# Windowed attention scores from 256-query strips and shared half tiles, in a two-layer transformer kernel on one Trainium2 core

## The chip, the cores and the metric

The kernel runs on one core of one Trainium2 chip. The metric is the device time of one execution in microseconds (us). A core has engines that run side by side and wait for one another by semaphores: TensorE (PE) multiplies matrices, ScalarE (ACT) does exponentials and GELU, VectorE (DVE) copies, adds and normalises, GpSimd (POOL) does masks and small work, SyncE (SP) issues the DMAs. PE's results go to PSUM, eight banks of 128 partitions x 512 float32.

## The reference

Two layers on x, 2048 tokens by 576, in bfloat16. Each layer adds an attention block and an MLP block, both behind a layer norm (each branch normalises twice on the MLP side):

```python
H = 32; Dh = D // H; W = 256            # 32 heads of 18
scores = jnp.einsum("bhqd,bhkd->bhqk", q, k) * (Dh ** -0.5)
mask = (idx[:, None] - idx[None, :] >= 0) & (idx[:, None] - idx[None, :] < W)
p = _softmax(jnp.where(mask[None, None], scores, -1e9), axis=-1)
o = jnp.einsum("bhqk,bhkd->bhqd", p, v)          # then @ wo
h = _gelu(jnp.einsum("bsd,df->bsf", y, w1) + b1) # F = 4608
return jnp.einsum("bsf,fd->bsd", h, w2) + b2
```

A query sees its own position and the 255 before it. Seen from a tile of 128 keys, the queries that matter run from the tile's first token to 255 tokens past its last: 384 queries, of which the first 128 and the last 128 are triangles.

## The kernel before, in words

The 2048 tokens are cut into chunks of 512 (four tiles of 128 queries). Two layers give eight chunks, k = 0 to 7. Per chunk there are: `qkv` (projections, L835 in the 64x128 array shape), `E` (attention, in three parts of 3, 3 and 2 head groups), `tail` (output projection, L1070), `G_part` (first MLP layer with GELU, three parts, L1115 and ACT L1125) and `mm2` (second MLP layer, three parts). The stages of chunk k's attention are interleaved with those of chunk k-1's MLP.

**Attention.** The 32 heads are eight groups g of four. A head has 18 channels in a 32-row strip, so four heads fill the array's rows: a score matmul (L923) has 32 rows and 128 columns of weights (a key tile), and the four of a group run side by side, each into its own PSUM bank. For a group, `units_of` lists three units of 512 score columns (six segments of 128, 256 or 384 queries, 12 blocks of 128 x 128 in all). A unit goes through `scores`: 8 matmuls, two exponentials (L933, two heads each, 1,024 elements a partition) into a slot of `pT` (six slots), and masks by affine_select on POOL (L954) over each diagonal or far-edge block. Chunks 0 and 4 start a layer, so they have no earlier tiles: nine blocks a group, and in chunk 4 the ninth blocks of four groups share one unit (`scores9`). `pv` (L975) multiplies the 12 blocks with V: 24 matmuls of 128 rows x 20 columns, four heads side by side, one PSUM bank for a group. V carries a column of ones, so the sum of a row comes with it, and DVE divides (L986 to L992). The first chunk has its own routine `E0`, which issues the first unit of three groups ahead.

**Array shapes.** PE's work comes in four shapes: full (128x128), 64-row halves (`qkv`, `tail`, `G_part`), 32-row quarters (scores) and 32-column quarters (`pv`). `mm2` may be issued as full matmuls (L775) or as four column quarters (L778, `quad`); it takes quarters where it stands in one run with `pv`, so that the shape need not change there.

**Order.** Nothing runs in source order. A planner (`Plan.schedule`) gives every task a cost and a latency written in the source, and picks the next by earliest start and then by priority; a change of shape costs `SWITCH`. A table `PL.nudge` adds a number to each stage's priority, and `PL.turn` holds back tasks that would change the shape. The result is one fixed instruction list per engine. Where the planner sees PE idle for over 0.4 us in the first 140 us, `keep_warm` puts in matmuls on a zero tile (L671), whose result nobody reads.

Of the kernel before, what the change touches and what calls it, by code (L numbers as in the profile page):

```python
# [8 lines left out]
ALU = mybir.AluOpType  # L9
# [426 lines left out]
def build_kernel(nc, A_x, A_wqkv, A_wo, B_x, B_w1, B_b1, B_w2, B_b2, out):  # L436
# [19 lines left out]
    PVG = [()] * 8  # L456
    PVLAG = 1
# [20 lines left out]
    PL.turn = {"hc": 0.3, "rh": 0.05, "rc": 0.05, "ch": 0.3}  # L478
    PL.nudge = {"": -1.63, "b": -20.47, "ea0.0": 108.12, "ea0.1": -112.05, "ea0.p0": -0.32, "ea0.p1": -13.77, "ea0.p2": -108.16,
# [333 lines left out]
    def qkv(k, i, prio0):  # L813
        l, t0, nt = CH[k]
        A = l * NT + t0 + i
        for n, w in enumerate("qkv"):
# [32 lines left out]
            else:  # L849
# [16 lines left out]
                if k == 0 and (w == "k"):  # L866
# [15 lines left out]
    def units_of(k):  # L882

        l, t0, nt = CH[k]
        if nt == 4:
# [3 lines left out]
        if t0 == 0:  # L889
            us = [[(0, 0, 3, 0)], [(1, 1, 3, 128)], [(2, 2, 2, 256), (3, 3, 1, 128)]]  # L890
# [467 lines left out]
```

## Time and profile before

| what | value |
|---|---|
| time, median of 3 runs | 856.21 us (855.98 to 856.74) |
| span of the profiled execution | 857.2 us |
| mean granted TensorE clock | 0.998 |
| PE busy, matmuls | 842.7 us, 12,180 |
| ACT busy | 599.1 us, of it exponentials (L933) 344.9 in 372 |
| POOL busy | 379.1 us, of it masks (L954) 282.8 in 370 |
| score matmuls (L923) | 1,248 in one group of the page, 63.2 us busy |
| PV matmuls (L975) | 1,440, 50.4 us busy |
| MLP matmuls (L1115; L775 and L778) | 291.8; 188.5 and 96.5 us busy |

The page gives no time for the profiled execution beside its span, which is 1.0 us above the median of the runs. The span is counted from the first instruction to the last. Rows of the timeline merge neighbouring instructions of one line; a row's second number reaches to the end of the last one, which lies under the first of the next row, since matmuls are pipelined. "PEld" are the weight loads, which run beside the matmuls. Matmul counts of the page may miss a few records; the listings of the program have 1,440 score matmuls.

### The profile page before, as it was taken

The page shows a single profiled execution, that of the slowest core. Times are in us where ns is not written, and L with a number is a line of the kernel's source. Part 1 is how long each engine was busy: PE and PEld are TensorE (multiplying, and loading weights), DVE is VectorE, ACT ScalarE, POOL GpSimd, SP SyncE. Part 2 cuts the span into 40 slices and gives each one's busy share as a digit, 9 for nine tenths or more (in the row PEclk, how much of TensorE's full clock was granted, in tenths as well). Part 3 has the DMA queues.
Part 4 walks back from the last instruction along what each step waited for, and adds up shares of the span by engine and source line. Part 5 has one row for each costly group of instructions (what it writes and reads, how often), then busy time and mean ns, then how long its engine had stood idle before and what let it go on. Part 6 is the DMA issues. An engine that isn't in the chain of part 4 may idle for free.

```text
span 857.2 us, 28212 instructions
## 1 busy us (share of the span) xinstructions
PE 842.7 (98%) x12180; PEld 517.6 (60%) x12180; DVE 398.6 (46%) x949; ACT 599.1 (70%) x745; POOL 379.1 (44%) x569
## 2 busy tenths in 40 slices
PE   8999999999999999999999999999999999999998
PEld 6555556556566565666665655656556556556556
DVE  6777434655257352672445723564226534162013
ACT  4988887778757787476773877748885689853730
POOL 4776554375235662263421654426534276322100
PEclk9999999999999999999999999999999999999999
DMA  7899435461596534967258443595345963346320
GB/s 198 195 184 149 127 124 145 115 165 45 166 182 124 154 94 121 186 133 191 85 124 195 89 149 122 104 223 130 112 157 116 225 187 109 119 133 186 116 84 29
DMA packets 181996, 119.86 MB, mean 140 GB/s; under 512 B 107504, under 2 KB 181872, under 8 KB 181872
## 3 DMA queue, kind: packets, MB, share of 16 engines
q1 hardware_dynamic: 181872, 118.05, 55.1%
q8 instruction: 96, 1.57, 0.8%
q14 instruction: 28, 0.23, 0.1%
HBM read 90.10 MB, written 2.36 MB: 108 GB/s over the span
## 4 chain that ended last, share of the span: by engine, by line
PE 91%; DMA 3%; DVE 2%; ACT 2%; POOL 1%; issue 1%; SPq 0%; DVEq 0%; POOLq 0%; ACTq 0%
PE ps L1115 31%; PE ps L775 25%; PE ps L778 11%; PE ps L835 8%; PE ps L923 6%; PE ps L975 5%; PE ps L1070 4%; DMA xnTm<-xn 2%; ACT pT L933 1%; DMA wqkv<-in_A_wqkv_dram 1%; PE ps L794 1%; DVE x_res L1047 1%; POOL pT L954 1%; DMA x_res<-qn 1%; DVE st_all L684 1%
## 5 line engine op out<-in xcount | busy, mean ns | idle before, releaser
L954 POOL TENSOR_SCALAR_AFFINE_SELECT pT<-pT 128x1024 bf16<-128x1024 bf16 (+1 forms) x370 | 282.8, 786 | 219.3 <-ACT pT L933 217.1
L933 ACT ACTIVATE pT<-ps 128x1024 bf16<-128x1024 f32 (+1 forms) x372 | 344.9, 999 | 42.4 <-PE ps L923 41.7
L1115 PE MATMUL ps<-xnTm,w_sb 64*128 64x512 bf16 x2592 | 291.8, 376 | 0.6 <-DVE x_res L1050 0.3
L1125 ACT ACTIVATE hT<-ps,b1col 128x512 bf16<-128x512 f32 x276 | 168.0, 688 | 176.5 <-PE ps L1115 176.4
L1115 PEld LDWEIGHTS ps<-xnTm,w_sb 64*128 64x128 bf16 x2592 | 127.5, 94 | 140.7 <-issue 4.0
L775 PE MATMUL ps<-w_sb,hT 128*128 128x288 bf16 x1410 | 188.5, 287 | 0.9 <-DVE vA L847 0.8
L1047 DVE TENSOR_TENSOR x_res<-ps,x_res 128x288 f32<-128x288 f32 x224 | 100.5, 454 | 180.7 <-PE ps L775 122.3
L775 PEld LDWEIGHTS ps<-w_sb,hT 128*128 128x128 bf16 x1410 | 130.5, 98 | 50.5 <-issue 16.9
L778 PE MATMUL ps<-w_sb,hT 128*32 128x288 bf16 x2808 | 96.5, 286 | 0.2
L835 PE MATMUL ps<-wqkv,xnTa 64*128 64x288 bf16 x1296 | 91.3, 283 | 2.2 <-DVE vA L847 0.9
L859 DVE CAST qn<-ps 128x288 bf16<-128x288 f32 x112 | 46.4, 451 | 86.4 <-PE ps L835 78.5
L986 DVE STREAM_TRANSPOSE oq<-ps 128x512 f32<-128x512 f32 x64 | 45.8, 716 | 84.6 <-PE ps L975 83.9
L778 PEld LDWEIGHTS ps<-w_sb,hT 128*32 128x32 bf16 x2808 | 72.5, 97 | 14.9 <-issue 3.4
L835 PEld LDWEIGHTS ps<-wqkv,xnTa 64*128 64x128 bf16 x1296 | 61.4, 94 | 30.0 <-issue 3.9
L923 PE MATMUL ps<-qT,kT 32*128 32x128 bf16 (+2 forms) x1248 | 63.2, 274 | 2.5 <-ACT pT L933 2.5
L697 POOL TENSOR_SCALAR vtmp<-mv_all 128x1 f32<-128x1 f32 (+2 forms) x45 | 9.2, 204 | 120.5 <-DVE mv_all L688 119.1
L1131 POOL TENSOR_TENSOR x_res<-x_res,b2bc 128x576 f32<-128x576 f32 x32 | 40.2, 1276 | 37.6 <-ACT hT L1125 37.4
L684 DVE BATCH_NORM_STATS2 st_all<-x_res 128x6 f32<-128x288 f32 (+1 forms) x128 | 53.5, 446 | 3.0 <-DMA x_res<-in_A_x_dram 2.1
L847 DVE CAST vA<-ps 128x288 bf16<-128x288 f32 x60 | 25.3, 448 | 55.1 <-PE ps L835 49.1
L975 PE MATMUL ps<-pT,vA 128*20 128x384 bf16 (+2 forms) x1440 | 50.4, 275 | 0.3 <-DVE vA L847 0.2
L923 PEld LDWEIGHTS ps<-qT,kT 32*128 32x128 bf16 x1248 | 19.2, 92 | 41.4 <-issue 26.9
L1070 PE MATMUL ps<-wo_sb,attT 64*128 64x288 bf16 x576 | 42.5, 283 | 0.3
(58 smaller groups left out, 478.4 us busy)
## 6 DMA issues: line engine op xcount, KB each, us to landing
w_sb<-in_B_w_dram SPq DMA_DIRECT2D x46, 864.0 KB, 6.1
w_sb<-in_B_w_dram SPq DMA_DIRECT2D x48, 768.0 KB, 4.8
w_sb<-in_B_w_dram SPq DMA_DIRECT2D x96, 48.0 KB, 4.6
wqkv<-in_A_wqkv_dram SPq DMA_DIRECT2D x3, 576.0 KB, 5.6
x_res<-in_A_x_dram SPq DMA_DIRECT2D x3, 576.0 KB, 4.3
wqkv<-in_B_w_dram SPq DMA_DIRECT2D x2, 864.0 KB, 5.2
out_dram<-x_res SPq DMA_DIRECT2D x12, 144.0 KB, 1.9
xnTm<-xn SPq DMA_TRANSPOSE x36, 2.8
```

The source lines that it names most:

```text
L684: add("dve", lambda e, i=i, s=s: e.bn_stats(st_all[:, t, i, :], s[:, t, i * HB:(i + 1) * HB]), reads=res, writes=[f"st{t}_{i}"], cost=0.37 ...
L775: return e.matmul(bank(b)[:, 0:HB], lhs, rhs, start=start, stop=stop, skip_group_check=True)
L778: ins = e.matmul(bank(b)[32 * j:32 * j + 32, 0:HB], lhs[:, 32 * j:32 * j + 32], rhs, start=start, stop=stop, tile_position=(0, 32 * j), sk ...
L835: ins = e.matmul(bank(bs[o])[:, 0:HB], xnTa[r:r + 64, c, i * 128:(i + 1) * 128], wqkv[r:r + 64, c, col:col + HB], start=(c == 4), stop=(ph ...
L923: ins = e.matmul(two(bs[j // 2])[:, j % 2, col:col + nq * 128], k_of(T0 + so)[0][32 * j:32 * j + 32, gg, :], qs[32 * j:32 * j + 32, gg, qo ...
L933: add("act", lambda e, h2=h2: e.activation(pT[:, sl, 2 * h2:2 * h2 + 2, lo:hi], two(bs[h2])[:, :, lo:hi], ACT.Exp, scale=SCALE), reads=[bs ...
L954: add("pool", lambda e, ap=ap, pat=pat, sgn=sgn, kind=kind: e.affine_select(ap, ap, pattern=pat, compare_op=(ALU.is_ge if kind == "d" else ...
L975: ins = e.matmul(bank(bo)[32 * j:32 * j + VW, qo * 128:(qo + nq) * 128], vA[:, (T0 + so) % VS, 8 * j + g, :], pT[:, sl, j, col:col + nq * ...
L1047: add("dve", lambda e: e.tensor_tensor(x_res[:, t, sl], bank(b)[:, 0:HB], x_old[:, t, sl], ALU.add), reads=[b] + ([f"xin{t}"] if first els ...
L1070: ins = e.matmul(bank(bs[o])[:, 0:HB], attT[r:r + 64, c, i * 128:(i + 1) * 128], wo_sb[r:r + 64, c, col:col + HB], start=(ph == 0 and c == ...
L1115: ins = e.matmul(bank(bks[i])[:, 0:n], w1_sb[r:r + 64, sls[i], col:col + 128], xnTm[r:r + 64, k % 2, c, 0:n], start=(c == 4), stop=(ph == ...
L1125: add("act", lambda e, ff=ff, hd=hd, bk=bk: e.activation(hd[:, 0:n], bank(bk)[:, 0:n], ACT.Gelu_apprx_tanh, bias=b1col[:, ff:ff + 1]), rea ...
```

## The change

**Scores.** A key tile meets only 256 queries in the full 128-key shape, from its own middle to the middle two tiles later. What is left are two triangles of 64 x 64: the tile's first 64 keys with its first 64 queries, and its last 64 keys with the 64 queries that follow the strip. The second triangle of tile i-2 and the first of tile i are put into the same 64 PSUM columns, one in partitions 0 to 63, the other in 64 to 127, by matmuls of 32 rows x 64 columns (eight side by side). Eight such pairs of triangles fill one unit, which serves two groups (four groups in chunks 0 and 4). A group then has 2.5 units of 512 columns and not 3 (chunks 0 and 4: 2.25 units, the first of 384 columns).

**Masks.** A shared unit takes two slots: POOL writes the far triangles with their mask into the second slot (`up`) and masks the near ones in place, so that each slot has zeros in the other half of the partitions. The 256-query strips have half-width triangles at both ends.

**PV.** It still runs over 128 partitions and the same columns per group (1,536; 1,152 in chunks 0 and 4): 6 segments of the two strip units and 8 segments of 64 columns from the two slots.

**Order.** A fifth shape "s" is known to the planner, with the cost `SSTEP` for its steps; `E`, `E0` and `pv` are rewritten for the new units, and the whole table of nudges is another one.

```diff
+    SSTEP = 0.045
-    PL.turn = {"hc": 0.3, "rh": 0.05, "rc": 0.05, "ch": 0.3}
-    PL.nudge = {"": -1.63, "b": -20.47, "ea0.0": 108.12, "ea0.1": -112.05, "ea0.p0": -0.32, "ea0.p1": -13.77, "ea0.p2": -108.16,
...
+    PL.turn = {"hc": 0.3, "rh": 0.05, "rc": 0.05, "ch": 0.3, "sh": 0.05, "sc": 0.05}
+    PL.nudge = {"": -251.12, "b": 5.46, "ea0.0": 2.43, "ea0.1": 0.99, "ea0.2": 1.23, "ea0.n0": 94.47, "ea0.p0": -189.64,
...
-            us = [[(0, 0, 3, 0), (-2, 0, 1, 384)], [(1, 1, 3, 128), (3, 3, 1, 0)], [(-1, 0, 2, 0), (2, 2, 2, 256)]]
...
+    def units_of(k, g):
+
+        if CH[k][1] == 0:
+            return [("", [(g, 0, 0, 5, 0), (g, 1, 2, 1, 320)]),
+                    (f"n{g}", [(g + n // 2, 2 + n % 2, 64 * n) for n in range(8)] if g % 4 == 0 else None),
+                    ("", [(g, 1, 3, 4, 0), (g, 2, 5, 3, 256), (g, 3, 7, 1, 448)])]
+        return [(f"n{g}", [(g + n // 4, n % 4, 64 * n) for n in range(8)] if g % 2 == 0 else None),
+                ("", [(g, 0, 1, 4, 0), (g, 1, 3, 4, 256)]),
+                ("", [(g, -1, 0, 3, 0), (g, -2, 0, 1, 192), (g, 3, 7, 1, 256), (g, 2, 5, 3, 320)])]
...
+                    if halves:
+                        gg, i, col = seg
+                        for h, so in ((0, i), (1, i - 2)):
+                            ins = e.matmul(two(bs[j // 2])[64 * h:64 * h + 64, j % 2, col:col + 64], k_of(T0 + so)[0][row, gg, 64 * h:64 * h + 64],
+                                           qs[row, gg, 64 * (2 * i + h):64 * (2 * i + h) + 64], start=True, stop=True, tile_position=(32 * j, 64 * h),
+                                           skip_group_check=True)
+                    else:
+                        gg, so, q, n, col = seg
+                        ins = e.matmul(two(bs[j // 2])[:, j % 2, col:col + 64 * n], k_of(T0 + so)[0][row, gg, :], qs[row, gg, 64 * q:64 * (q + n)],
+                                       start=True, stop=True, tile_position=(32 * j, 0), skip_group_check=True)
...
+    def visit(k, g, segs, prio):
+        sl = scores(k, segs, prio)
+        hs = [f"p{sl}h0", f"p{sl}h1"]
+        if len(segs[0]) == 3:
+            up = slots.popleft()
+            gs = sorted({x[0] for x in segs})
+            for n, gg in enumerate(gs):
+                cols = [x[2] // 64 for x in segs if x[0] == gg]
+                mask(sl, up, cols, -64, -1, hs, f"p{up}m{n}", prio)
+                mask(sl, sl, cols, 0, 1, hs + [f"p{up}m{n}x"], f"p{sl}m{n}", prio)
...
+            for n, (so, q, nq, sl, col) in enumerate(todo):
                 for j in range(4):
+                    ins = e.matmul(bank(bo)[32 * j:32 * j + VW, 64 * q:64 * (q + nq)], vA[:, (T0 + so) % VS, 8 * j + g, :],
+                                   pT[:, sl, j, col:col + 64 * nq], start=(n == 0), stop=(n == len(todo) - 1),
```

**Where the order moves.** PE's list at the start of chunk 6's attention: L923 are scores, L775 and L778 the second MLP layer of chunk 4 or 5, L835 projections for the next chunk. Before:

```order
L835 MATMUL ps<-wqkv,xnTa 128x288 x36
L923 MATMUL ps<-qT,kT 128x384 x4
L923 MATMUL ps<-qT,kT 128x128 x4
L775 MATMUL ps<-w_sb,hT 128x288 x24
L923 MATMUL ps<-qT,kT 128x384 x4
L923 MATMUL ps<-qT,kT 128x128 x4
L835 MATMUL ps<-wqkv,xnTa 128x288 x36
L923 MATMUL ps<-qT,kT 128x256 x8
L775 MATMUL ps<-w_sb,hT 128x288 x12
```

With the change, at the same place (L923 is now the 32x64 shape, L928 the strips, L786 the full second layer, L846 the projections):

```order
L846 MATMUL ps<-wqkv,xnTa 128x288 x36
L923 MATMUL ps<-qT,kT 64x64 x64
L786 MATMUL ps<-w_sb,hT 128x288 x12
L928 MATMUL ps<-qT,kT 128x256 x8
L786 MATMUL ps<-w_sb,hT 128x288 x12
L928 MATMUL ps<-qT,kT 128x192 x4
L928 MATMUL ps<-qT,kT 128x64 x8
L928 MATMUL ps<-qT,kT 128x192 x4
L786 MATMUL ps<-w_sb,hT 128x288 x12
```

The chunk now opens with the shared unit of groups 0 and 1, 64 short matmuls; a group then has two score runs between the MLP's pieces where it had three.

The first PV groups of the same chunk, before (L975 is PV):

```order
L975 MATMUL ps<-pT,vA 20x384 x4
L975 MATMUL ps<-pT,vA 20x128 x4
L975 MATMUL ps<-pT,vA 20x384 x4
L975 MATMUL ps<-pT,vA 20x128 x4
L975 MATMUL ps<-pT,vA 20x256 x8
L778 MATMUL ps<-w_sb,hT 32x288 x24
```

And with the change (L1025 is PV, L789 the quartered second layer):

```order
L789 MATMUL ps<-w_sb,hT 32x288 x24
L1025 MATMUL ps<-pT,vA 20x256 x8
L1025 MATMUL ps<-pT,vA 20x192 x4
L1025 MATMUL ps<-pT,vA 20x64 x8
L1025 MATMUL ps<-pT,vA 20x192 x4
L1025 MATMUL ps<-pT,vA 20x64 x32
L789 MATMUL ps<-w_sb,hT 32x288 x24
L923 MATMUL ps<-qT,kT 64x64 x64
```

A PV group has 56 matmuls where it had 24, 40 of them 64 columns wide, and a shared unit of 64 short matmuls stands one small piece of the MLP behind it.

Over the whole program PE's list has 16,366 matmuls where it had 12,180: 3,264 score and 3,264 PV matmuls for 1,440 and 1,440, 1,513 full and 3,644 quartered ones of the second layer (with chunk 1's projections) for 1,687 and 2,948, and 36 filler matmuls for the 20 of L671. The shape changes 344 times, before 393 times.

More of the change, by code (lines that the diff above doesn't have):

```diff
@@ L916, in scores @@
         bs = [Bank(SC, True), Bank(SC, True)]
+        halves = len(segs[0]) == 3
         def fn(e):
             ins = None
[L920 to L921 removed]
+            for seg in segs:
                 for j in range(4):
[L923 to L925 removed]
@@ L926, in fn @@
-            return ins
-        rd = [f"{qname}{qo + i}" for (so, qo, nq, col) in parts for i in range(nq)] + [k_of(T0 + p[0])[1] for p in parts]
-        ncol = sum(p[2] for p in parts) * 128
-        add("pe", fn, reads=rd, writes=bs, cost=0.01 + ncol * 0.00042, prio=prio, lat=0.15, alloc=bs, fifo="pa", mode="r", after=[f"p{sl}h{h}" for h in range(2)] + [f"p{sl}m{m}" for m in range(3)])
-        lo = min(p[3] for p in parts)
-        hi = max(p[3] + p[2] * 128 for p in parts)
+                    row = slice(32 * j, 32 * j + 32)
@@ L932, in scores @@
+        add("pe", fn, reads=list(dict.fromkeys(rd)), writes=bs, cost=cost, prio=prio, lat=0.15, alloc=bs, fifo="pa", mode="s" if halves else "r",
+            after=[f"p{sl}h{h}" for h in range(2)] + [f"p{sl}{m}" for m in MS])
         for h2 in range(2):
@@ L957, in scores, with runs_of @@
-        return sl
-    def pv(k, g, units, bo, first, last, prio):
-        slots.extend(sl for _, sl in units)
-        if k in SHARE and last:
-            units = units + [ninth[k, g]]
-            if g % 4 == 3:
-                slots.append(ninth[k, g][1])
+        return sl
+    def runs_of(cols):
+        out = []
+        for c in cols:
+            if out and (len(out[-1]) == 1 or c - out[-1][-1] == out[-1][1] - out[-1][0]) and not (len(out[-1]) == 1 and c - out[-1][0] > 1 and c + 1 in cols):
+                out[-1].append(c)
+            else:
+                out.append([c])
+        return out
@@ new lines, in collect @@
+    def collect(k, g, prio):
+        parts, free = [], []
+        for name, segs in units_of(k, g):
+            if name:
+                if segs is not None:
+                    kept, PL.part = PL.part, f".{name}"
+                    visit(k, g, segs, prio)
+                    PL.part = kept
+                    yield None
+                continue
+            p, f = visit(k, g, segs, prio)
+            parts += p
+            free += f
+            yield None
+        sp, ssl, n, end = side[k, g]
+        yield parts + sp, free, ssl, n, end
@@ L966, in pv @@
+    def pv(k, g, what, bo, prio):
+        todo, free, ssl, sn, end = what
+        slots.extend(free + (ssl if end else []))
         l, t0, nt = CH[k]
```

141 lines of the change are left out of this document (57 added, 84 removed), and 134 rows, old and new, of the table add.

## The prediction

> **What bounds the kernel now.** I read the page's header and slices first, then the chain of waits, then the windows by stage, then the timeline of TensorE inside one attention stage.
>
> ```profile
> span 857.2 us, 28212 instructions
> PE 842.7 (98%) x12180; PEld 517.6 (60%) x12180; DVE 398.6 (46%) x949; ACT 599.1 (70%) x745; POOL 379.1 (44%) x569
> PE 91%; DMA 3%; DVE 2%; ACT 2%; POOL 1%; issue 1%; SPq 0%; DVEq 0%; POOLq 0%; ACTq 0%
> ```
>
> TensorE (PE) sets the end: 98% busy, and 91% of the chain that ended last. A busy PE still hides gaps, so the windows come next (columns: span, then PE, weight loads, DVE, ACT, POOL busy, granted clock).
>
> ```profile
> 20.00:56.40 36.40, 32.90 (x479) 19.15 (x479) 26.74 (x67) 35.10 (x50) 28.34 (x44) 1.00 0.93 185
> 56.40:60.00 3.60, 3.60 (x49) 1.89 (x49) 2.09 (x5) 1.42 (x3) 1.91 (x4) 0.53 1.01 270
> 60.00:86.00 26.00, 24.18 (x390) 14.87 (x390) 19.02 (x47) 21.48 (x33) 17.14 (x33) 1.00 0.89 148
> 86.00:200.00 114.00, 113.66 (x1654) 66.53 (x1650) 52.19 (x126) 90.21 (x111) 58.65 (x83) 1.00 0.48 134
> 200.00:400.00 200.00, 199.92 (x3066) 123.20 (x3060) 99.73 (x235) 141.38 (x169) 93.57 (x137) 1.00 0.59 138
> 400.00:600.00 200.00, 198.25 (x3170) 123.88 (x3166) 98.40 (x232) 139.70 (x166) 86.47 (x132) 1.00 0.57 138
> 600.00:740.00 140.00, 139.18 (x2054) 83.38 (x2052) 52.39 (x117) 108.06 (x133) 65.83 (x86) 1.00 0.54 151
> ```
>
> From 86 to 740 us PE stands idle for 0.34 + 0.08 + 1.75 + 0.82 = 3.0 us in all. There only less PE work, or fewer changes of array shape, can gain. From 20 to 56.4 us ACT is busy 35.10 of 36.40 us and PE idles 3.5 us: the first chunk's attention is bound by the exponentials. At 56.4 us the clock falls to 0.53 for 3.6 us.
>
> The timeline of PE in chunk 6, whose chain of waits also gives one long run:
>
> ```profile
> 576.93 3.10 PE L775 MATMUL ps<-w_sb,hT 128*128 128x288 bf16 x24 [0.80 <-DVE vA L847]
> 579.97 0.40 PE L923 MATMUL ps<-qT,kT 32*128 32x384 bf16 x8
> 584.51 0.40 PE L923 MATMUL ps<-qT,kT 32*128 32x384 bf16 x8
> 584.84 1.64 PE L775 MATMUL ps<-w_sb,hT 128*128 128x288 bf16 x12
> 586.42 0.40 PE L923 MATMUL ps<-qT,kT 32*128 32x384 bf16 x8
> 586.74 0.83 PE L975 MATMUL ps<-pT,vA 128*20 128x384 bf16 x24
> 587.40 0.91 PE L778 MATMUL ps<-w_sb,hT 128*32 128x288 bf16 x24
> ```
> ```profile
> 240.72 4.52 PE ps L778 x144
> 771.75 11.87 PE ps L775 x96
> 783.62 23.42 PE ps L1115 x216
> 818.90 11.76 PE ps L1115 x108
> 830.66 23.64 PE ps L775 x192
> ```
>
> I price PE from start to next start. 24 full matmuls of 288 columns take 579.97 - 576.93 = 3.04 us, 96 of them 11.87; so one takes (11.87 - 3.04)/72 = 122.6 ns, and **one change of array shape** 3.04 - 24 x 0.1226 = 0.10 us. 54 pairs of 512 columns take 11.76 us, less one change 11.66, or 215.9 ns a pair. Two sizes give a **column** (215.9 - 122.6)/224 = 0.4165 ns and a **step** (matmuls that run side by side in the array) 2.7 ns more. Checks: a score unit, 512 columns, takes 0.33 us (0.213 + 0.10 + 0.013 at its second step); a PV group, 1,536 columns in 6 steps, 0.66 (0.640 + 0.016).
>
> **The change, part by part.** The counts are from the listings of the two programs.
>
> *Fewer score columns.* 360 steps with 92,160 columns become 368 steps in the 32x128 shape (63,488 columns) and 224 in the 32x64 shape (14,336, eight matmuls side by side): 77,824. 14,336 x 0.4165 ns = **-6.0 us**.
>
> *Fewer changes of shape.* The new order changes the shape 344 times, not 393, though each of the 28 shared tiles needs a shape of its own. 49 x 0.10 = **-4.9**. 174 second-layer steps go from one full matmul to four quarters: 36 quarter steps took 4.52 us with one change, 122.8 ns each against 122.6, so nothing.
>
> *More steps.* PV streams the same 92,160 columns, but in 816 steps for 360; scores have 232 more. 688 x 2.7 ns = **+1.8**.
>
> *Short steps.* 128 score steps and 576 PV steps have 64 columns, and 224 are half tiles. No row shows a step under 128 columns with several tiles. From below: 64 x 0.4165 + 2.7 = 29.4 ns. From above: the 128-column step, 56.0 ns, +26.6 each. For the instructions' pace I take the weight loads at the head of one score unit:
>
> ```profile
> 575.73 0.12 PEld L923 LDWEIGHTS ps<-qT,kT 32*128 32x128 bf16 x8 [0.24 <-issue]
> L923 PEld LDWEIGHTS ps<-qT,kT x1248: 90/91/113, 19.8 to 750.6; 32*128 32x128 bf16 x179
> ```
>
> Eight loads span 0.12 us and one lasts 0.09, so they start within some 30 ns, with four matmuls among them: 12 instructions, 2.5 ns each. A PV or score step has 8 instructions, 20 ns, below 29.4. A half-tile step has 16, 40 ns: 224 x (40 - 29.4) = **+2.4**. I add **+0.8** for the other 704 (1.2 ns each, near the lower end because the pace leaves room). Bounds for all 928: 0 to +24.7.
>
> [...]
>
> *Instruction fetch.* PE issues 2 x 16,366 instructions for 2 x 12,180.
>
> ```profile
> q8 instruction: 96, 1.57, 0.8%
> 586.00:596.00 10.00, 10.00 (x178) 6.26 (x178) 5.16 (x11) 9.31 (x11) 7.46 (x10) 1.00 0.32 50
> ```
>
> 96 packets carry 24,360 PE instructions, about 254 each; a packet's time is 0.008 x 16 x 857.2/96 = 1.14 us. Where 178 matmuls and their loads fill 10 us, a packet lasts 7 us. In the new order 64 half-tile matmuls next to a PV group of 56 are 240 instructions in some 1.1 us. If the fetch falls behind there, the loss is at most 0.25 us at each of 28 shared tiles, 7 us. I take **+1.5**. [...]
>
> *ACT.* 372 exponentials become 312.
>
> ```profile
> L933 ACT ACTIVATE pT<-ps 128x1024 bf16<-128x1024 f32 x324 | 309.7, 1023 | 38.9 <-PE ps L923 38.7
> L933 ACT ACTIVATE pT<-ps 128x768 bf16<-128x768 f32 x48 | 35.3, 837 | 3.5 <-PE ps L923 3.0
> 31.87 15.97 ACT L933 ACTIVATE pT<-ps 128x768 bf16<-128x768 f32 x22 [0.81 <-PE ps L923]
> PE ps L923 <- ACT pT L933: 2.9, 10, 0.4
> PEld ps L923 <- ACT pT L933: 13.8, 45, 0.7
> ```
>
> 44 x 1.023 + 16 x 0.837 = 58 us of ACT go, but PE waited for exponentials only 2.9 us (13.8 more are weight loads beside running matmuls), so after 86 us this is worth about nothing. In chunk 0 the pace is 15.97/22 = 0.73 us; 48 x 0.73 = 35 become 16 x 0.73 + 20 x 0.91 (1.023 less the same overlap of 0.11) = 30: 5 us off the bound engine. PE idles 3.5 us there, so no more can return, and the order puts 16 more filler matmuls (those of L671) into the first chunks, which stand where the planner saw PE without work. I take **-1.7**; bounds -7 (all idle and the low clock gone: 3.5 + 1.8 + 3.6 x 0.47) and +3 (new idle as long as before's 3.0 us from 86 us on).
>
> *POOL.* The masks cover the same 245,760 elements a partition in 416 selects for 370.
>
> ```profile
> L954 POOL TENSOR_SCALAR_AFFINE_SELECT pT<-pT 128x512 bf16<-128x512 bf16 x264 | 167.1, 648 | 189.1 <-ACT pT L933 188.1
> L954 POOL TENSOR_SCALAR_AFFINE_SELECT pT<-pT 128x1024 bf16<-128x1024 bf16 x104 | 115.8, 1113 | 28.7 <-ACT pT L933 27.6 <-PE ps L923 0.4
> PEld ps L975 <- POOL pT L954: 1.3, 6, 0.2
> ```
>
> 512 elements cost 648 ns, 512 more 465, so 183 ns are fixed and 46 selects add 8 us to an engine at 44%. PV waited for masks 1.3 us in all: cover is there, and if it went, 64 PV groups would wait.
>
> **Sum.** -6.0 - 4.9 + 1.8 + 2.4 + 0.8 + 1.5 - 1.7 = -6.1. The profiled execution's span is 857.2 us, so 851.1 there; it lies 1.0 above the median of the runs, 856.2. Forecast: **850 us**.
>
> **The rivals.**
> *Slower: short steps are bound by loads or issue, not by columns* (place: PV's 576 and the scores' 128 steps). Without its 0.8 the sum is -6.9; 6.9/704 = 9.8 ns more each, 39 ns a step, wipe it out. At 56 ns the 704 cost 18.7, the half tiles 3.6 more than taken: -6.9 + 18.7 + 3.6 = +15.4, 872 us. For it: no row has such a step. Against: PV's 128-column steps pay 2.7 ns, not more. Chance 0.13.
> *Fetch lags at every shared tile:* 5.5 more than taken, -0.6, 856: no change. For it: 218 instructions per us in such places against 36 in the window. Against: nothing in before waits for it. 0.13.
> *The start gains all it can:* 5.3 more, 845. For it: ACT's 35.10 of 36.40. Against: the added fillers. 0.17.
> *POOL becomes the pace.* In 586 to 596 us ACT is busy 9.31 and POOL 7.46 of 10; with a sixth of the exponentials gone the same masks come in 8.3 us, POOL at 90%. If each of 64 PV groups waits 0.12 us, +7.7: 858. 0.07.
>
> **How the numbers follow.** The forecast's own case, 846 to 854.4, has 0.50. A difference under 0.2% (854.5 to 857.9) cannot be told from none. Faster: 0.47 of the forecast, 0.17 start, 0.02 of fetch = 0.66. Same: 0.03 + 0.09 + 0.02 = 0.14. Slower: 0.13 of the short steps, 0.02 of fetch, 0.05 of POOL = 0.20. Range: 843 (most of the start's gain) to 861, where short steps at about 46 ns would lie (704 x 17 = 12 less 6.9); about 0.07 lies below and 0.10 above.
>
> **What would show it.** Right: PV groups take 0.68 us start to next start, half-tile runs 0.42 with their change, PE idle after 86 us stays near 3 us, ACT loses some 58 us without moving the end. Wrong: PV groups of 0.9 us or more (the slower rival); PE gaps put down to issue inside half-tile or PV runs (fetch); PV's weight loads waiting for POOL by more than 8 us (POOL).

## The result, and the profile after

The changed kernel takes 883.17 us (median of four runs, 882.06 to 888.30) where the kernel before takes 856.13 beside it: ratio 1.0325, 95% interval 1.0298 to 1.0352. It is slower by 27 us; the forecast was 850 us. The profiled executions' spans, 880.4 and 857.2 us, differ by 23.2 us, and that is what is accounted for below. Where a run lists both, its span lies some 1.7 us under its time (880.4 of 882.06; for the kernel before 854.8 of 856.5), so the profiled execution of before, with its low clock at 56.4 us, was some 2.7 us above its median, not 1.0, and that of the changed kernel 1.1 us below its own, which makes up the 27.

The page's header and chain of the changed kernel, and its DMA queue of the kind "instruction" (packets, MB, share):

```profile
span 880.4 us, 36408 instructions
PE 850.1 (97%) x16366; PEld 560.1 (64%) x16366; DVE 402.0 (46%) x949; ACT 549.0 (62%) x685; POOL 393.3 (45%) x615
PE 86%; DMA 5%; DVE 3%; issue 2%; ACT 2%; POOL 1%; SPq 1%; ACTq 0%; POOLq 0%
q8 instruction: 129, 2.11, 1.0%
```

ACT has 50 us less work, as the change intends, and TensorE still sets the end. But its share of the chain fell from 91% to 86%, and "issue", time in which an engine waits for nothing that the profile shows, rose to 2%. The windows (span, then PE, weight loads, DVE, ACT, POOL busy, granted clock):

```profile
60.00:86.00 26.00, 22.72 (x450) 13.51 (x452) 18.11 (x47) 14.55 (x20) 15.44 (x30) 0.87 0.83 151
86.00:200.00 114.00, 109.74 (x2227) 70.71 (x2221) 53.38 (x122) 83.65 (x104) 65.79 (x93) 1.00 0.55 128
200.00:400.00 200.00, 193.60 (x4018) 131.25 (x4016) 96.33 (x230) 121.00 (x146) 82.94 (x125) 1.00 0.57 133
400.00:600.00 200.00, 198.39 (x4121) 130.51 (x4110) 98.38 (x230) 125.60 (x157) 88.84 (x148) 1.00 0.58 141
600.00:740.00 140.00, 135.81 (x2911) 89.94 (x2912) 54.37 (x121) 94.89 (x115) 71.29 (x92) 1.00 0.61 148
```

Taken from the windows' spans less PE's busy time, PE stands idle from 86 to 740 us for 4.26 + 6.40 + 1.61 + 4.19 = 16.5 us where it was 3.0, at full clock, with DMA at about the share it had. PE's waits (us in total, times, longest) name what for:

```profile
PE ps L789 <- issue: 5.5, 8, 1.1
PE ps L928 <- issue: 3.7, 4, 2.4
PE ps L1025 <- issue: 2.7, 4, 1.4
PE ps L923 <- DMA kT<-qn: 2.2, 1, 2.2
PE ps L923 <- issue: 1.6, 2, 0.9
PEld ps L1025 <- POOL pT L962: 1.2, 4, 0.4
```

13.5 us are "issue", in 18 waits of up to 2.4 us. The kernel before has no such row for PE's matmuls. The timeline at two of them:

```profile
290.30 0.85 PE L1025 MATMUL ps<-pT,vA 128*20 128x256 bf16 x56
291.08 0.75 PE L923 MATMUL ps<-qT,kT 32*64 32x64 bf16 x64
291.76 0.54 PE L789 MATMUL ps<-w_sb,hT 128*32 128x288 bf16 x9
293.25 0.67 PE L789 MATMUL ps<-w_sb,hT 128*32 128x288 bf16 x15 [0.95 <-issue]
293.64 0.96 PE L1025 MATMUL ps<-pT,vA 128*20 128x256 bf16 x56
...
713.37 0.78 PE L1025 MATMUL ps<-pT,vA 128*20 128x256 bf16 x45
715.55 0.26 PE L1025 MATMUL ps<-pT,vA 128*20 128x64 bf16 x11 [1.40 <-issue]
```

A PV group of 56 and a half-tile run of 64 go by, 240 instructions in 1.46 us, and then PE stops in the midst of 24 second-layer matmuls that wait for nobody; at 715 us it stops within a PV group. I numbered PE's instructions (loads, matmuls and semaphore instructions) in the order of the program: after 86 us each stop over 0.15 us without a semaphore is before an instruction 190 to 192 places into a block of 256. 129 packets for 2 x 16,366 loads and matmuls are 254 each, so a block looks like a packet of that queue (2.11 MB / 129 = 16.4 KB). The packet that ends last before PE goes on at 293.25 us ends at 291.98, and at all 16 stops over 0.15 us without a semaphore after 86 us PE goes on 1.23 to 1.52 us after a packet's end. So it looks as if PE stands still because its instructions have not arrived.

**The account.** For every run of matmuls of one line, I took its time to the next start, less its price by the prediction's own rates (column 0.417 ns, step 2.7 ns, change of shape 98 ns, 10.5 ns more for a score run). The price is a count times these rates and not a measurement; the excess is what the profile has beyond it. The sums, in us of the profiled execution:

| kernel | priced work | excess before 94 us | excess of half-tile runs | other excess | ahead of the first and behind the last | span |
|---|---|---|---|---|---|---|
| before | 808.7 | 15.1 | none | 5.8 | 27.6 | 857.2 |
| after | 800.9 | 20.7 | 9.3 | 21.9 | 27.6 | 880.4 |

The saving is there: 7.8 us less priced work, with the half-tile steps at their lower price of 29.4 ns. Against it stand +5.6 at the start, +9.3 in half-tile runs (1.9 of it two stops for instructions) and +16.1 elsewhere, mostly such stops (14 of them, 11.4 us of "issue"): -7.8 + 5.6 + 9.3 + 16.1 = +23.2.

### The profile page after: what moved, and what is told of

It reads as the page before. It is cut to its first block, busy times and chain, and to the rows that moved or that the text cites. A ratio compares the mean times of both kernels' runs of the same rounds, so it can differ in the third digit from the quotient of the medians.

```text
span 880.4 us, 36408 instructions
## 1 busy us (share of the span) xinstructions
PE 850.1 (97%) x16366; PEld 560.1 (64%) x16366; DVE 402.0 (46%) x949; ACT 549.0 (62%) x685; POOL 393.3 (45%) x615
## 3 DMA queue, kind: packets, MB, share of 16 engines
q8 instruction: 129, 2.11, 1.0%
## 4 chain that ended last, share of the span: by engine, by line
PE 86%; DMA 5%; DVE 3%; issue 2%; ACT 2%; POOL 1%; SPq 1%; ACTq 0%; POOLq 0%
PE ps L1156 31%; PE ps L786 19%; PE ps L789 13%; PE ps L846 9%; PE ps L1025 5%; PE ps L928 4%; PE ps L1111 3%; DMA xnTm<-xn 2%; PE ps L923 2%; ACT pT L941 1%; PE ps L805 1%; DVE x_res L1088 1%; DVE st_all L695 1%; SPq L634 1%; POOL pT L962 1%
## 5 line engine op out<-in xcount | busy, mean ns | idle before, releaser
L962 POOL TENSOR_SCALAR_AFFINE_SELECT pT<-pT 128x512 bf16<-128x512 bf16 (+2 forms) x416 | 298.0, 751 | 231.9 <-ACT pT L941 231.3
L941 ACT ACTIVATE pT<-ps 128x1024 bf16<-128x1024 f32 (+1 forms) x312 | 293.6, 1001 | 96.9 <-PE ps L928 73.2
L786 PE MATMUL ps<-w_sb,hT 128*128 128x288 bf16 x1236 | 164.1, 287 | 0.1
L786 PEld LDWEIGHTS ps<-w_sb,hT 128*128 128x128 bf16 x1236 | 114.9, 98 | 38.6 <-issue 8.4
L789 PE MATMUL ps<-w_sb,hT 128*32 128x288 bf16 x3504 | 121.4, 287 | 5.5 <-issue 5.5
L789 PEld LDWEIGHTS ps<-w_sb,hT 128*32 128x32 bf16 x3504 | 93.3, 96 | 18.2 <-issue 8.6
L846 PE MATMUL ps<-wqkv,xnTa 64*128 64x288 bf16 x1296 | 94.9, 287 | 2.6 <-DVE x_res L1088 0.9
L846 PEld LDWEIGHTS ps<-wqkv,xnTa 64*128 64x128 bf16 x1296 | 61.5, 95 | 31.3 <-PE ps L846 3.0
L1025 PE MATMUL ps<-pT,vA 128*20 128x64 bf16 (+3 forms) x3264 | 53.3, 214 | 3.1 <-issue 2.7
L1025 PEld LDWEIGHTS ps<-pT,vA 128*20 128x20 bf16 x3264 | 47.7, 92 | 11.2 <-issue 5.5
L928 PE MATMUL ps<-qT,kT 32*128 32x64 bf16 (+3 forms) x1280 | 44.3, 237 | 5.0 <-issue 3.7
L726 DVE TENSOR_SCALAR xn<-x_res,mv_all,rstd 128x576 bf16<-128x576 f32 (+1 forms) x60 | 34.2, 574 | 25.8 <-DMA xnTm<-xn 15.4
```

The source lines that it names most:

```text
L786: return e.matmul(bank(b)[:, 0:HB], lhs, rhs, start=start, stop=stop, skip_group_check=True)
L789: ins = e.matmul(bank(b)[32 * j:32 * j + 32, 0:HB], lhs[:, 32 * j:32 * j + 32], rhs, start=start, stop=stop, tile_position=(0, 32 * j), sk ...
L846: ins = e.matmul(bank(bs[o])[:, 0:HB], xnTa[r:r + 64, c, i * 128:(i + 1) * 128], wqkv[r:r + 64, c, col:col + HB], start=(c == 4), stop=(ph ...
L928: ins = e.matmul(two(bs[j // 2])[:, j % 2, col:col + 64 * n], k_of(T0 + so)[0][row, gg, :], qs[row, gg, 64 * q:64 * (q + n)], start=True, ...
L941: add("act", lambda e, h2=h2: e.activation(pT[:, sl, 2 * h2:2 * h2 + 2, lo:hi], two(bs[h2])[:, :, lo:hi], ACT.Exp, scale=SCALE), reads=[bs ...
L962: add("pool", lambda e, nb=nb, at=at: e.affine_select(dst_[:, :, at, :], src_[:, :, at, :], pattern=[[0, 4]] + ([[0, nb]] if nb > 1 else [ ...
```

## The experiments

The theory from this profile: **fetch**. PE stops where a block of 256 of its instructions runs faster than the next one arrives. Rivals: the 64-column steps themselves are dear (the prediction's slower rival); the half-tile steps are bound by their weight loads; the new order loses time by its waits. An edit moves the line numbers a little: the quartered second layer is L789 in the changed kernel, L790 in the first experiment and L778 in the kernel before.

**The same work at another place in the blocks.** The filler matmuls, 36 of 256 columns, become 108 of 128 and 64 columns; the computation and the order stay.

```diff
-            ins = e.matmul(bank(bk)[:, 0:256], warm[:, :], warm[:, :].unsqueeze(1).to_broadcast([P, 2, P]), start=True, stop=True)
+            for c0, c1 in ((0, 128), (128, 192), (192, 256)):
+                ins = e.matmul(bank(bk)[:, c0:c1], warm[:, :], warm[:, 0:c1 - c0], start=True, stop=True)
```

> The changed kernel, with each of its 36 filler matmuls of 256 columns issued as three (128, 64 and 64 columns): 72 more matmuls, 144 more PE instructions, 0.56 of a 256-instruction block, all before 71 us; nothing else differs. Theory 'fetch' (PE's instructions come in blocks of 256, and the engine runs dry at a block's end where the block before was consumed too fast): the stalls without a semaphore leave the matmuls at which they stand now (185.3, 212.8, 293.2, 353.7, 503.2, 611.0, 711.0, 715.6, 742.5 us) and stand at other matmuls, again 256 x n instructions apart at the same phase of the count (0.75); 10 to 20 us in all, time 873 to 890. Theory 'place' (something in those runs themselves, banks or loads, makes them stall): the same matmuls stall by the same time; 883.

Measured: 902.85 us (898.94 to 903.85), ratio to the kernel before 1.0533, interval 1.0507 to 1.0559. 144 instructions in the first 90.1 us (not 71, as expected), whose columns are the same, cost 20 us. The timeline of this kernel at one of its largest stops:

```profile
565.03 0.86 PE L1026 MATMUL ps<-pT,vA 128*20 128x256 bf16 x56
565.78 0.91 PE L790 MATMUL ps<-w_sb,hT 128*32 128x288 bf16 x22
568.83 1.77 PE L790 MATMUL ps<-w_sb,hT 128*32 128x288 bf16 x50 [2.15 <-issue]
```

The stops stand before other matmuls than in the changed kernel, and again 190 to 192 places into a block. PE's "issue" rows sum to 25.6 us (13.1 + 7.6 + 2.5 + 2.4) for 13.5, and two more have grown:

```profile
PE ps L1157 <- DMA xnTm<-xn: 3.5, 2, 2.4
PE ps L847 <- DMA xnTa<-xn: 2.3, 2, 1.3
```

These waits for transposed inputs were 0.8 us together in the changed kernel. And the clock takes part. The stops that end at 683.67 and 735.91 us last 2.19 and 2.66 us, and at each the granted clock falls to 0.50 for 3.4 us, 1.7 us of clock lost each time (windows as above):

```profile
684.70:688.10 3.40, 3.40 (x28) 1.81 (x24) 1.07 (x3) 1.94 (x2) 1.71 (x3) 0.50 0.03 5
735.90:739.30 3.40, 3.39 (x91) 2.67 (x90) 0.66 (x2) 0.00 (x0) 2.32 (x3) 0.50 0.15 48
```

This profile has 13.6 us at half clock, the changed kernel's 6.8 us (all from 70.0 us on, at its longest wait for a DMA). Stops 12.1 us longer, transposes 5.0 and clock 3.4 are 20.5 of the 21.8 us between the two spans. So the place in the block decides where PE stops, not the operation. The size was expected at 10 to 20 us of stalls and up to 890 us; both came out higher.

**The PV segments alone.** The kernel before, with PV cut into the changed kernel's 14 steps a group; the scores, the masks and the order are those of before.

```diff
+        def cuts(so, qo, nq):
+            a, b = 2 * qo, 2 * (qo + nq)
+            at = [a] + [x for x in (2 * so + 1, 2 * so + 5) if a < x < b] + [b]
+            return [(x - a, y - x) for x, y in zip(at, at[1:])]
...
-                    ins = e.matmul(bank(bo)[32 * j:32 * j + VW, qo * 128:(qo + nq) * 128], vA[:, (T0 + so) % VS, 8 * j + g, :],
+                    ins = e.matmul(bank(bo)[32 * j:32 * j + VW, 64 * q:64 * (q + w)], vA[:, (T0 + so) % VS, 8 * j + g, :],
```

> The kernel before, with its PV groups cut into the segments of the change (14 steps for 6 in most chunks, the same columns; 456 more steps in all), everything else and the order as before. Theory 'steps are cheap, fetch is not': 456 x 2.7 ns = +1.2 us, and as the 3,600 more PE instructions make some blocks of 256 shorter than 3.7 us, 1 to 6 us of stalls without a semaphore; 857 to 863. Rival 'short steps cost as much as 128-column ones' (the prediction's slower rival): 64-column steps at 56 ns, +15 us, 871. If neither steps nor fetch cost: 857.

Measured: 869.61 us (868.37 to 872.35), ratio 1.0161, interval 1.0136 to 1.0186: 13.5 us slower. The total is what the rival asked, its cause is not: the timeline

```profile
436.17 1.19 PE L980 MATMUL ps<-pT,vA 128*20 128x64 bf16 x88
437.19 2.99 PE L778 MATMUL ps<-w_sb,hT 128*32 128x288 bf16 x90
441.50 0.42 PE L778 MATMUL ps<-w_sb,hT 128*32 128x288 bf16 x6 [1.32 <-issue]
```

shows two PV groups of chunk 4, 2,304 columns in 22 steps, 16 of these of 64 columns. By the prediction's column and step they take 0.96 + 0.06 = 1.02 us, and they do; at 56 ns each the 64-column steps would make it 1.45. PE stops 3.0 us later, among second-layer matmuls of 288 columns. Ten stops like this are 8.8 us of "issue" (4.8 + 2.2 + 1.8), or 10.5 us as excess over the price. By the account the spans' 10.2 us are +1.3 of priced work, +10.0 of other excess and -1.0 at the start. So the steps cost what the theory says, but the stops were expected at 1 to 6 us, 857 to 863 us in all, and are more. Shared score tiles are not needed for such a loss, PV's instructions alone bring it.

**One triangle for two.** The changed kernel, with the far triangles' scores left out (the near ones as 32x128 steps of 64 columns), so that a shared unit has 32 matmuls for 64.

```diff
-                        for h, so in ((0, i), (1, i - 2)):
-                            ins = e.matmul(two(bs[j // 2])[64 * h:64 * h + 64, j % 2, col:col + 64], k_of(T0 + so)[0][row, gg, 64 * h:64 * h + 64],
-                                           qs[row, gg, 64 * (2 * i + h):64 * (2 * i + h) + 64], start=True, stop=True, tile_position=(32 * j, 64 * h),
+                        ins = e.matmul(two(bs[j // 2])[:, j % 2, col:col + 64], k_of(T0 + i)[0][row, gg, :],
+                                       qs[row, gg, 128 * i:128 * i + 64], start=True, stop=True, tile_position=(32 * j, 0),
```

> The changed kernel, leaving out the far triangles' scores: a shared unit multiplies only the near tile, with all 128 keys in the 32x128 shape, 32 matmuls of 64 columns in place of 64 in the 32x64 shape; exponentials, masks, PV and the order stay. Theory 'a shared unit's run is bound by the pace at which instructions are handed out, 8.3 ns for a load and its matmul': the run falls from 0.71 us to 8 steps x 33 ns + 0.1 = 0.37, 28 x 0.34 = -9.5 us; 1,792 fewer PE instructions take some stalls of the fetch away, -2 to -8; time 865 to 871. Rival 'the runs cost what was forecast (0.42 us) and the loss lies elsewhere': -28 x 0.05 = -1.4, 881.

Measured: 867.33 us (865.87 to 871.37), ratio 1.0134, interval 1.0107 to 1.0162, 16 us under the changed kernel, as the theory has it. By the account (spans 880.4 and 869.6 us) the half-tile excess of 9.3 is gone and the start's falls by 4.4, while the other excess is 2.6 higher: "issue" still has 9.0 us (5.2 + 2.4 + 1.2 + 0.2), and PV's instructions are all there.

**What a short step costs by itself.** Behind the last work of the kernel before come series of 96 matmuls, each between 48 full ones: half tiles over eight, four and two positions of the array, 32x128 score steps, PV steps, and at last 1,024 PV steps' matmuls. All have 64 columns, and nobody reads them.

```diff
+        def strips(n, rows, halves):
+            for _ in range(n // (rows * halves)):
+                for j in range(rows):
+                    for h in range(halves):
+                        e.matmul(bank(bk[j])[64 * h:64 * h + 64, 0:64], warm[32 * j:32 * j + 32, 0:64], warm[32 * j:32 * j + 32, 0:64],
+                                 start=True, stop=True, tile_position=(32 * j, 64 * h), skip_group_check=True)
...
+        wide(48)
+        strips(96, 4, 2)
+        wide(48)
+        strips(96, 2, 2)
...
+        pvs(96)
+        wide(48)
+        return pvs(1024)
```

> The kernel before, and behind its last matmul a series of matmuls on zeros that nobody reads: 96 each in the 32x64 shape over 8, 4 and 2 tiles of the array, 96 in the 32x128 shape, 96 in PV's shape, all of 64 columns, each behind 48 full matmuls of 256; then 1,024 in PV's shape without a break. Theory 'pace of instructions': in the later part of each short series a load and its matmul take 8.3 ns, so a step takes 67 ns over 8 tiles, 33 over 4, and 29 (the columns) over 2; 33 in the 32x128 and PV shapes. Rival 'a load of 64 columns holds its tile': 67 ns a step over 8, 4 and 2 tiles alike. Theory 'fetch': the 1,024 take about 3.7 us for each 128 of them, 30 us, in spurts; without a limit of the fetch 1,024 x 8.3 = 8.5 us. The span is 857 + 6 x 5.4 + 5 + 30 = 925, or 903 without that limit.

Measured: 920.36 us, one run. The timeline of the tail:

```profile
858.00 0.97 PE L1318 MATMUL ps<-warm 32*64 32x64 bf16 x96
858.90 5.41 PE L1312 MATMUL ps<-warm 128*128 128x256 bf16 x48
...
870.50 1.70 PE L1318 MATMUL ps<-warm 32*64 32x64 bf16 x96
872.13 5.41 PE L1312 MATMUL ps<-warm 128*128 128x256 bf16 x48
877.48 0.95 PE L1324 MATMUL ps<-warm 32*128 32x64 bf16 x96
878.36 5.42 PE L1312 MATMUL ps<-warm 128*128 128x256 bf16 x48
...
893.89 1.21 PE L1330 MATMUL ps<-warm 128*20 128x64 bf16 x128 [2.29 <-issue]
897.63 1.89 PE L1330 MATMUL ps<-warm 128*20 128x64 bf16 x128 [2.53 <-issue]
```

Less one change of 0.10 us, 12 half-tile steps over eight positions take 0.80 us, **66.7 ns** each; 48 steps over two positions take 1.53 us, 31.9 ns each; 24 score steps 0.78 us, 32.5 ns. A pair of a load and a matmul thus takes 8.1 to 8.3 ns, 4.1 per instruction, over four positions and over eight and with loads of 20, 64 and 128 columns; over two positions a pair takes 16 ns, and there the step of 31.9 ns is near the 29.4 priced for its columns. The 64-column loads don't bind: with two positions each reloads every 31.9 ns, not every 66.7. What a half-tile step pays is 16 instructions, 4.2 ns each. And the last series stops before every 128 matmuls, with 3.74 to 4.02 us from one resumption to the next. From 895.9 us on the granted clock is 0.50 and 128 matmuls take 1.89 us for 1.21; the time between resumptions hardly changes, so PE's own work does not set it.

**The threshold.** The kernel before, and behind it 512 matmuls each in PV's shape of 128, 256 and 384 columns; nobody reads them.

```diff
+        for w in (128, 256, 384):
+            for _ in range(128):
+                for j in range(4):
+                    ins = e.matmul(bank(bk[0])[32 * j:32 * j + VW, 0:w], warm[:, 0:VW], warm[:, :].unsqueeze(1).to_broadcast([P, w // 128, P]),
+                                   start=True, stop=True, tile_position=(0, 32 * j), skip_group_check=True)
```

> The kernel before, and behind its last work three series of 512 matmuls in PV's shape (128 rows x 20 columns, four side by side) of 128, then 256, then 384 columns. Theory (fetch: a block of 256 PE instructions takes 3.75 us at least): each 128 matmuls take 3.75 us at 128 columns, where their work is 32 x 56 ns = 1.8 us, with a stall of some 2 us in every block; 3.75 at 256 columns (work 3.5), a stall of 0.2 to 0.3 us; 5.2 us at 384 columns (32 x 162.6 ns), no stall. Some 15 + 15 + 21 us of tail, 908 us in all. Rival (the stalls belong to the 64-column steps, not to the instruction count): 1.8, 3.5 and 5.2 us without stalls, 899 us.

Measured: 905.63 us, one run, nearer the theory's 908 than the rival's 899. The tail's timeline, up to the resumption in the second series:

```profile
854.80 2.35 PE L1313 MATMUL ps<-warm 128*20 128x128 bf16 x156
858.52 1.97 PE L1313 MATMUL ps<-warm 128*20 128x128 bf16 x128 [1.37 <-issue]
861.99 1.97 PE L1313 MATMUL ps<-warm 128*20 128x128 bf16 x128 [1.51 <-issue]
865.74 2.71 PE L1313 MATMUL ps<-warm 128*20 128x128 bf16 x128 [1.78 <-issue]
869.48 33.91 PE L1313 MATMUL ps<-warm 128*20 128x256 bf16 x968 [1.03 <-issue]
```

At 128 columns, 128 matmuls are 1.8 us of work and take 3.47, 3.75 and 3.74 us. At 256 columns (3.50 us of work) the single starts show blocks of 3.74, 3.49 and 3.72 us; at 384 columns 5.20 each, with no stop. **In these rows of short matmuls a block of 256 PE instructions takes 3.5 to 4.0 us, with 1.8 us of work and with 1.2** (3.47 to 3.75 here, 3.74 to 4.02 in the series before this one). The packet records say of what that is made. From 855 to 870 us four packets of instructions last 1.14 us on average (1.9% of 16 engines' 15 us), and three of them start 0.9 to 1.4 us after PE went on. At the changed kernel's 16 stops the packet lasts 0.92 to 1.55 us, and PE goes on 1.23 to 1.52 us after its end.

The start of a packet is not fixed. In the changed kernel many packets start earlier, some up to 2.0 us before PE has begun the block ahead of theirs, and 11 blocks go by in 2.50 to 3.48 us without a stop. For the shortest, from 775.64 to 778.14 us, the packet starts 0.14 us after PE enters the block, lasts 1.11 us, and PE uses it 1.25 us after its end; in the changed kernel's profile that last time is never under 1.2 us. So a single short block can pass; in the two added rows none does. What sets a packet's start stays open.

**Fewer PV instructions.** The changed kernel; a group's eight 64-column segments become two of 256 columns (chunks 0 and 4: four become two). Most of these segments then meet another tile's V and another query's place; columns, waits and order stay.

```diff
-            for n, (so, q, nq, sl, col) in enumerate(todo):
+            wide = []
+            for x in todo:
+                p = wide[-1] if wide else None
+                if x[2] == 1 and p and p[5] and p[3] == x[3] and p[4] + 64 * p[2] == x[4]:
+                    p[2] += 1
+                else:
+                    wide.append([*x, x[2] == 1 and x[3] in ssl])
...
+            for n, (so, q, nq, sl, col, _) in enumerate(wide):
```

> The changed kernel; PV's eight 64-column segments of a group from the shared slots are issued as two segments of 256 columns (chunks 0 and 4: four as two of 128), with the same columns, the same waits and the same order of the list; this leaves out the right V tile and query place of six (two) of the segments. A PV group then has 32 matmuls, not 56. Theory (fetch: a block of 256 PE instructions that lasts under 3.3 to 3.7 us makes PE wait): from the changed kernel's own trace 7 to 10 blocks stay under that, short by 5 to 9 us, where 18 to 25 were; so 8 to 13 us of its 14 to 17 us of stalls go, and 6 steps x 2.7 ns x 64 groups = 1 us: 867 to 874 us beside 883. Rival (the 64-column steps themselves cost 40 ns or more): 384 steps go, 10.6 ns of each with them, 4 us and 1 us: 878. Rival (the loss is the order's, waits and switches): 881 to 883.

Measured: 874.94 us (871.38 to 877.24), ratio 1.0208, interval 1.0177 to 1.0240, 1 us over the theory's range and 3 under the nearest rival. The "issue" rows sum to 5.2 us (1.7 + 1.2 + 1.1 + 1.0 + 0.2) for 13.5, as the theory asks, but other rows have grown:

```profile
PE ps L846 <- DMA xnTa<-xn: 2.8, 2, 2.0
PE ps L1166 <- DMA xnTm<-xn: 2.4, 1, 2.4
```

PE now comes to the next chunk's projections and to an MLP piece sooner, and the transposes of the normalised input are not there yet.

**Both.** The last kernel, with the far triangles' scores left out too (the two edits above).

> The kernel with PV's wide side segments, and its far triangles' scores left out too (the near ones as 32x128 steps of 64 columns): 32 matmuls in a shared unit for 64. Theory (fetch): no block but some 5 stays under 3.7 us, 0 to 3 us of stalls; the half-tile runs' excess of 8 us goes too. The changed kernel's span of 880.4 less 14, 8 and 1: 854 to 861 us, so what is left against the kernel before is the start's loss (+5) and the saved columns and shape changes (-8). Rival (losses outside the instruction count, in the order): 868 or more, as the two edits would not add up.

Measured: 862.87 us (860.48 to 864.74), ratio 1.0079, interval 1.0061 to 1.0096. Its waits:

```profile
PE ps L846 <- DMA xnTa<-xn: 3.5, 2, 1.9
PE ps L1165 <- DMA xnTm<-xn: 2.9, 2, 2.4
PE ps L789 <- issue: 1.1, 2, 0.6
PE ps L927 <- issue: 0.6, 1, 0.6
```

With 14,190 matmuls the fetch costs 1.7 us, and 20 us of the 27 are back. Yet it is still 6 us behind the kernel before, and 2 over what I expected: by the account above its priced work is 8.3 us under that of before, the start's excess is 3.9 over it, and the other excess 6.1 over it. Of these 10.0 us the two transposes' rows are 6.4. (The account's two spans, 858.8 and 857.2 us, differ by less than the times do.) That the fetch stops had covered them fits, but two of these waits stand in the shifted kernel too, which has more stops; what sets them stays open.

**Fewer instructions for more work.** The changed kernel with its whole computation; the second MLP layer is always issued as full matmuls, also beside PV.

```diff
-            if all(x.wide is not None for x in run):
-                for x in run:
+            for x in run:
+                if x.wide is not None:
                     x.wide[0] = True
```

> The changed kernel, the whole computation, the same order; only the second MLP layer (and chunk 1's projections) are issued as one full matmul for every four column quarters. The columns and steps stay; PE has 2,733 matmuls less (13,633 for 16,366), and 73 changes of shape more (417 for 344). Theory (fetch): 73 x 0.098 = +7.2 us for the shapes; from the changed kernel's own trace 8 to 12 blocks of 256 instructions stay under 3.3 to 3.7 us, short by 4 to 8 us, where 18 to 25 were short by 13 to 23, so 9 to 15 us of stalls go: 2 to 8 us faster than the changed kernel, 875 to 881 us, although the price of the work itself rises. Rival (stalls do not hang on the instruction count): the shape changes alone, 889 to 891 us.

Measured: 877.87 us (875.38 to 879.90), ratio 1.0246, interval 1.0221 to 1.0272, which lies wholly under that of the changed kernel; the time is within the theory's 875 to 881. Page and waits:

```profile
PE 853.5 (97%) x13633; PEld 544.4 (62%) x13633; DVE 401.9 (46%) x949; ACT 548.6 (63%) x685; POOL 393.0 (45%) x615
PE ps L786 <- issue: 2.1, 1, 2.1
PE ps L928 <- issue: 1.1, 1, 1.1
```

73 shape changes more make the priced work 7.1 us longer, and still the kernel is 5 us faster, since the "issue" rows fall from 13.5 to 3.2 us. This tells the instruction count apart from all that the attention's edits also change: no matmul of scores or PV was touched.

**The start.** In the changed kernel chunk 1's first shared unit waits for the last transposed k tile:

```profile
66.53 1.66 PE L846 MATMUL ps<-wqkv,xnTa 64*128 64x288 bf16 x20
70.38 0.23 PE L923 MATMUL ps<-x_res,xnTm 32*64 32x64 bf16 x1 [2.19 <-DMA kT<-qn]
```

In the experiment that unit takes tiles 0 and 1 for 2 and 3 (half its triangles are left out, the others done twice).

```diff
+                        i = i % 2 if k == 1 and segs[0][0] == 0 else i
                         for h, so in ((0, i), (1, i - 2)):
...
+        if halves and k == 1 and segs[0][0] == 0:
+            t.reads = tuple(dict.fromkeys([f"{qname}{x[1] % 2}" for x in segs] + [k_of(T0 + x[1] % 2 - y)[1] for x in segs for y in (0, 2)]))
```

> The changed kernel; the first shared unit of chunk 1 takes tiles 0 and 1 for its tiles 2 and 3 (half of its triangles left out, the others twice), so that it need not wait for the last two transposed k and q tiles; order and instruction count stay. Theory (the start's loss is this wait of 2.2 us and the lower clock behind it): the wait before the unit at 70.4 us falls under 0.5 us, the clock stays above 0.95 from 70 to 78 us, and 3 to 5 us go: 878 to 880 beside 883. Rival (the tiles are late for the next units too, so the wait moves on by one unit): within 1 us of the changed kernel, 882 to 884.

Measured: 881.33 us (877.36 to 887.76), ratio 1.0294, interval 1.0243 to 1.0345: between the theory and the rival, and not told apart from the changed kernel. Its windows and one row of its timeline:

```profile
70.00:78.00 8.00, 7.06 (x122) 4.29 (x120) 6.11 (x17) 6.31 (x9) 6.24 (x8) 1.00 1.14 209
78.00:94.00 16.00, 13.71 (x321) 8.15 (x321) 8.66 (x21) 13.63 (x18) 13.73 (x27) 0.89 0.89 178
84.66 0.83 PE L682 MATMUL ps<-warm 128*128 128x256 bf16 x6 [1.67 <-DVE qn L870]
```

The wait is gone and the clock is whole from 70 to 78 us (in the changed kernel it was 0.57 there), but 14 us later PE waits 1.67 us for DVE, and the clock is 0.89 from 78 to 94. The excess before 94 us falls from 20.7 to 18.8 only. So the wait is a part of the start's loss and the low clock is not bound to it; what else makes up the rest stays open.

The profiled execution took 887.76 us at a mean granted clock of 0.992: the clock falls again at fetch stops of 2.04 us (352.15) and 2.66 us (715.13). Two executions at a clock of 1.0 took 877.36 and 879.05 us, near what the theory asks. But the changed kernel's own four have clocks of 0.996 to 0.992, so its time at a clock of 1.0, and with it the worth of the wait alone, is not known.

## Why the prediction was wrong

*Fewer columns, fewer shape changes, more steps, short steps of four (-6.0 - 4.9 + 1.8 + 0.8).* Right, as far as the account can tell: the priced work fell by 7.8 us, and behind the start, outside half-tile runs and stops, the profile lies some 8 us above the price where before it lay 5.8. A PV group takes 0.78 us with the change of shape behind it (290.30 to 291.08), so 0.68, as the prediction named. The slower rival, 56 ns a step, did not happen; a long series pays 32.5 ns, a little over the 29.4 and 1.2 taken.

*The half-tile step, 40 ns (+2.4).* The mechanism, 16 instructions' pace, was right; the size was wrong, and so was the bound of 56 ns. 66.7 ns each make the runs 0.30 us longer than at 29.4, 28 runs 8.4 us where 2.4 were taken. The step that failed is the pace of 2.5 ns per instruction, read from the loads at the head of one score unit. The changed kernel's own runs show why the head misled: in the run at 291.08 us the first 32 matmuls start within 0.17 us, and after a pause of 0.07 us the rest come at 8.3 ns a pair. Why the head is faster, no run tests; it does not tell the pace, at any rate. The loads do not explain the 66.7 ns: over two positions a step with 64-column loads takes 31.9 ns.

*Instruction fetch (+1.5, bound 7).* This is the step that failed most: 13.5 us by the page's rows, and most of the 16.1 + 1.9 of the account. I compared a packet's 1.14 us with the time that the instructions run, and charged the lag at the 28 shared tiles alone. What counts is the whole round, 3.5 to 4.0 us per 256 instructions in the added rows of short matmuls: a packet of 1.14 us there, 1.23 to 1.52 us until PE goes on (by the changed kernel's stops), 0.9 to 1.4 until the next packet starts. And it counts everywhere, since PV's 112 instructions in 0.7 us, or four column quarters for one full matmul, also make a block short. By the changed kernel's starts, with the stops taken out, some 18 blocks lie under 3.3 us and 25 under 3.7, short by about 13 and 23 us; before has none under 3.7. So the fetch rival had the right mechanism at a chance of 0.13 with 856 us as its price; with the measured round its price would have been some 13 to 23 us for 7.

*174 second-layer steps go to column quarters: nothing.* Right by its duration, wrong by its instructions. With all 911 quartered steps back in full matmuls the kernel is 5 us faster although 73 shape changes come with it; the 174 alone were not tried.

*ACT and the start (-1.7, bounds -7 and +3).* ACT lost 50 us (58 forecast) and nothing of it moved the end. The start lost 5.6 us, beyond the bound of +3. From 60 to 86 us the clock is 0.87, 26 x 0.13 = 3.4 us of clock for 3.6 x 0.47 = 1.7 before. The end of the low clock, a part of the lower bound, was not to be had: 19 of the 21 runs of the kernel before beside the experiments have a granted clock of 1.0 as it is. And the shared unit needs all four tiles of its chunk: 2.2 us of wait. The order shown ahead of the prediction has the shared unit at the head of its chunk, and the prediction didn't ask what it waits for.

*POOL (0).* Right: PV's wait for masks is 1.2 us.

*What would show it.* The sign "PE gaps put down to issue" came, though mostly outside the half-tile and PV runs, for which I had named it: PE stops where it is 190 to 192 places into a block of 256, whatever stands there.

## What to carry to other kernels

Count instructions as a resource. On PE here, blocks of 256 consecutive instructions (128 loads and matmuls) that followed one another took 3.47 to 4.02 us each with 1.2 or 1.8 us of work, and 5.20 us, without a stop, where the work alone takes that long, though single ones of 2.50 to 3.48 us passed; and in a row of short matmuls each pair took 8.1 to 8.3 ns, but for the first 32 of the run read above (0.17 us). An edit that cuts columns by cutting matmuls into small pieces has to be checked against both over windows of the program, not per stage; a stop then shows as "issue" at a matmul that is not to blame.

## What was not expected of the hardware

- In the added rows of short matmuls 256 PE instructions took 3.47 to 3.75 us at 128 columns (1.8 us of work) and 3.74 to 4.02 us at 64 (1.2 us). Moving all instructions by 144 places cost 20 us with the same work.
- PE took a load and a matmul every 8.1 to 8.3 ns over four or eight positions of the array; 64 columns over two positions took 31.9 ns a step, near the 29.4 priced for the columns.
- A long fetch stop can cost more than its length. Eight stops of over 2 us stand in these profiles, outside the added series (2.15, 2.19 and 2.66 us in the first experiment, 2.44 in the changed kernel, 2.4 with one triangle, 2.04 and 2.66 in the experiment on the start, 2.1 with the full second layer); at six of them the granted clock falls to 0.50, for 3.4 us (once 6.8). It did not at the stop of 2.44 us in the changed kernel (353.71), nor at one of 2.15 us in the first experiment (568.83).
- The times of the changed kernel scatter more, 882.06 to 888.30 us where the kernel before lies within 855.98 to 856.74. They follow the granted clock: 0.996, 0.994, 0.994 and 0.992 for 882.06, 883.15, 883.20 and 888.30 us, which is 3.5 to 7 us of clock lost. What decides when it falls, no run tested.
